# Reordering the opening loads and the first pairs' schedule of a fused attention and feed-forward kernel

## The chip, the cores and the metric

The kernel runs on one core of one Trainium2 chip. The metric is device microseconds of that core, from the run's own clock; the span in the profile, from the first to the last instruction, is 1.7 to 2.1 us shorter in most runs. All runs quoted here are fast runs, with a mean granted clock of 0.990 to 1.000. The kernel before takes 418.2 us.

The engines' names in the profile: PE is TensorE's matmuls, PEld its weight loads, DVE is VectorE, ACT is ScalarE, POOL is GpSimd and SP is SyncE; PEq, ACTq and SPq are sequencers, which issue DMAs among other things.

## The reference

```python
# q, k, v: (8 batches, 8 heads, 576, 64); bias_table: (32 buckets, 8 heads)
scores = scale * np.matmul(q, k.transpose(0, 1, 3, 2))
...                                   # bucket = function of |i - j| only
bias = bias_table[bucket]
scores = scores + bias.transpose(2, 0, 1)[None, :, :, :]
attn = softmax(scores)                # written out in the original
x = (attn @ v).transpose(0, 2, 1, 3).reshape(4608, 512)
a = x @ moe_w_a                       # 512 x 1536
b = x @ moe_w_b
return (a * b) @ moe_w_out            # 1536 x 512
```

## The kernel before

The work is cut into 32 "pairs" of heads, four to a batch. For each pair, TensorE turns q and k (transposes), makes four 128-row blocks of scores (`qk1`) and the scores of the last 64 rows (`qk_tail`). ScalarE takes their exponential (`ex`, `ex_tail`), VectorE multiplies by the exponentiated bias `W` (`mul`), TensorE multiplies by the values (`av`), VectorE divides by the row sums (`norm`). From pair 4 on, slices of the feed-forward part, called units (`U`), are put between these steps. The order on every engine is fixed by the program.

The program uses eight banks of PSUM: two score tiles of two banks each (`ps_sc`), one for value products (`AV`), one for transposes (`TR`), two for the feed-forward part (`FF`). The exponentials go into a ring of eight tiles.

```python
atp   = ctx.enter_context(tc.tile_pool(name="atp", bufs=8))      # exponentials
ps_sc = ctx.enter_context(tc.tile_pool(name="ps_sc", bufs=2, space=PSUM))
...
nc.sync.dma_start(out=bt_sb[0:NB, :], in_=bias_table)            # bias table first
nc.scalar.dma_start(out=oh_sb[0:NB, :], in_=oh_handle.ap())      # one-hot of the buckets
make_identity(nc, id32[:, :])
...
load32(0, q, q32, (nc.sync, nc.scalar))                          # pair 0
load32(0, k, k32, (nc.sync, nc.scalar))
...
warm_up(5)
nc.tensor.matmul(out=tps[0:H, 0:NR], lhsT=bt_sb[0:NB, :], rhs=oh_sb[0:NB, :], ...)
warm_up(3)
nc.scalar.activation(out=tab_sb[...], in_=tps[...], func=ACTF.Exp)
nc.scalar.dma_start(out=tab.ap(), in_=tab_sb[0:H, :])            # to HBM ...
load_w(nc.gpsimd, 0)                                             # ... and back as W
...
for s in (1, 2):                       # pairs 1 and 2, still without feed-forward
    if s > 1:
        ex(s, 0)
    mul(s - 1, 3); mul_tail(s - 1)
    q_next(s);  qk1(s, 2); ex(s, 1)
    k_next(s);  qk1(s, 3); ex(s, 2)
    tails_next(s + 1, 1, ACT)          # last 64 rows of the next pair
    qk_tail(s); mul(s, 0)
    av(s - 1, 0); av(s - 1, 1); av(s - 1, 2); norm(s - 1, 0)
    mul(s, 1);  ex(s, 3)
    av(s - 1, 3, FF)
    qk1(s + 1, 0)                      # the next pair's first scores
    ex_tail(s); av(s - 1, 4); norm(s - 1, 3)
    mul(s, 2);  qk1(s + 1, 1)
...
# pairs 5 to 11, one step list each
    steps += [lambda: qk(s, 2), lambda: ex(s, 2)]
    if e:
        steps += [lambda: t_q(s + 1, TR), lambda: c_q(s + 1)]
    steps += [U, lambda: ex(s, 3), U, lambda: mul(s, 2)]
    if e:
        steps += [lambda: t_k(s + 1, TR), lambda: c_k(s + 1)]    # same bank as qktt
```

The softmax here doesn't subtract the row's maximum and nothing guards it: scores larger than these inputs give would overflow.

Of the kernel before, what the change touches and what calls it, by code (L numbers as in the profile page):

```python
# [13 lines left out]
def kernel(  # L14
# [11 lines left out]
    nc = tc.nc  # L26
# [6 lines left out]
    NB = 32  # L33
# [132 lines left out]
        eng.dma_start(out=W_sb[hp][:, :, :],  # L166
                      in_=bass.AP(tensor=tab, offset=2 * hp * TB, ap=[[1, 128], [TB, 2], [1, 384]]))

    nc.sync.dma_start(out=bt_sb[0:NB, :], in_=bias_table)
    nc.scalar.dma_start(out=oh_sb[0:NB, :], in_=oh_handle.ap())  # L170
    make_identity(nc, id32[:, :])
    def pad(eng, x, n):
        eng.memset(x[0:64, :, 1, 0:n], 0.0)
# [6 lines left out]
    def load32(p, src, out, engs):  # L180
        for h in range(2):
            load_h(engs[h], src, out[:, p, :, h, :], 0, 2 * p + h)

    load32(0, q, q32, (nc.sync, nc.scalar))
    load32(0, k, k32, (nc.sync, nc.scalar))
    load32(1, q, q32, (nc.sync, nc.sync))
    load32(1, k, k32, (nc.sync, nc.sync))

# [64 lines left out]
    def copy(eng, out, in_):  # L253
        if eng is nc.scalar:
            nc.scalar.activation(out=out, in_=in_, func=ACTF.Copy)
        else:
            nc.vector.tensor_copy(out=out, in_=in_)  # L257
# [21 lines left out]
    def bank(where, dt, name):  # L279
        return where[0].tile([128, 512 if dt is FP32 else 1024], dt, tag=where[1], name=name)  # L280
# [5 lines left out]
    def t_q(p, where):  # L286
        if p >= NP or not early(p // 4):
            return
        ps = bank(where, BF16, f"trq{p}")
        for t in range(NM):  # L290
            nc.tensor.transpose(ps[:, 128 * t:128 * t + 128], blocks(qn, p)[:, t, :, :], ident)  # L291
        st[p]["q"] = ps
# [13 lines left out]
    def t_k(p, where):  # L306
        if p >= NP or not early(p // 4):
            return
        ps = bank(where, BF16, f"trk{p}")
        for t in range(NM):  # L310
            nc.tensor.transpose(ps[:, 128 * t:128 * t + 128], blocks(kn, p)[:, t, :, :], ident)
        if p > 4:
            t_tails(p, ps, SM)
        st[p]["k"] = ps
# [265 lines left out]
    def t32(ps, src, p, t):  # L580
        nc.tensor.transpose(ps[:, 128 * t:128 * t + 128], src[:, p, t, :, :], id32[:, :])

    psk0, psq0 = bank(FF, FP32, "trk0a"), bank(TR, FP32, "trq0a")
    psq1, psk1 = bank(AV, FP32, "trq0b"), bank(FF, FP32, "trk0b")
    t32(psk0, k32, 0, 0)
    for t in range(NM):
        t32(psq0 if t < 2 else psq1, q32, 0, t)
    copy(ACT, QT[0][:, 0:256], psq0[:, 0:256])
    copy(None, KT[0][:, 0:128], psk0[:, 0:128])
    for t in range(1, NM):  # L590
        t32(psk1, k32, 0, t)
    copy(None, QT[0][:, 256:512], psq1[:, 256:512])
    copy(None, KT[0][:, 128:SM], psk1[:, 128:512])
    qk1(0, 0)
    qk1(0, 1, 1)
# [35 lines left out]
    load32(3, k, k32, (nc.sync, nc.sync))  # L631
    qk1(0, 3)
    ex(0, 2)
    tails_next(0, 2, None)
    qk1(1, 0)
    ex(0, 3)
    ex(1, 0)
    qk_tail(0)
# [5 lines left out]
    for s in (1, 2):  # L644
        if s > 1:
            ex(s, 0)
        mul(s - 1, 3)
        mul_tail(s - 1)
        q_next(s)
        qk1(s, 2)  # L650
        ex(s, 1)
        k_next(s)
        qk1(s, 3)
        ex(s, 2)
        tails_next(s + 1, 1, ACT)
        qk_tail(s)
        mul(s, 0)
        av(s - 1, 0)
        av(s - 1, 1)
        av(s - 1, 2)  # L660
        norm(s - 1, 0)
        mul(s, 1)
        ex(s, 3)
        av(s - 1, 3, FF)
        qk1(s + 1, 0)
        ex_tail(s)
        av(s - 1, 4)
        norm(s - 1, 3)
        mul(s, 2)
        qk1(s + 1, 1)  # L670
# [18 lines left out]
    ex(3, 2)  # L689
    av(2, 3, FF)  # L690
    av(2, 4)
    c_x(1)
    norm(2, 3)
    ex_tail(3)
    qk1(3, 3)
    mul(3, 0)
    ex(3, 3)
    t_x(2, FF)
    mul(3, 1)
    av_part(3, 0)  # L700
    c_x(2, ACT)
    t_q(4, FF)
    c_q(4, ACT)
    mul(3, 2)
    av_part(3, 1)
    mul_tail(3)
    av_part(3, 2)
    av_part(3, None)
    mul(3, 3)
    av_part(3, 3)  # L710
    t_k(4, FF)
    c_k(4, ACT)
    norm(3, 0)
    norm(3, 3)
# [1 line left out]
    t_x(3, AV, range(3))  # L716
    t_x(3, AV, range(3, 5))
    ff_mm(0, 0, wb_sb, "pb", 0, 3)
    c_x(3)

    def tails4():
        ps = bank(TR, BF16, "trt4")
# [15 lines left out]
    for s in range(4, NP + 1):  # L738
        new = s < NP
        U = "unit"  # L740
        A = lambda *jq: (lambda: [av(s - 1, j, AV if j < 3 or s >= R3 else TR) for j in jq])
        N = lambda j: (lambda: norm(s - 1, j))
        steps = []
        if s == R3:
            ring3 = True
        if s == 4:
            steps += [U, U, lambda: qk1(4, 0), lambda: ex(4, 0), lambda: qk1(4, 1), U, lambda: ex(4, 1),
                      lambda: qk1(4, 2), U, lambda: ex(4, 2), lambda: qk1(4, 3), lambda: ex(4, 3),
                      lambda: mul(4, 0), U, tails4, U, lambda: qk_tail(4), lambda: ex_tail(4),
                      lambda: mul(4, 1), U, lambda: mul(4, 2), U, lambda: mul(4, 3),  # L750
                      lambda: mul_tail(4), U, lambda: t_q(5, TR), lambda: c_q(5), U,
                      lambda: t_k(5, TR), lambda: c_k(5), U, U]
        elif new:
            e = early((s + 1) // 4)
            steps += [lambda: qk(s, 0), lambda: ex(s, 0), U, lambda: ex(s, 1), A(0, 1, 2), N(0), U,
                      lambda: mul(s, 0)]
            av34 = [A(3, 4), N(3)]
            if s - 1 in XD:
                av34 += [lambda: t_x(s - 1), lambda: turns(s)]
            if s < R3:  # L760
                steps += av34
            steps += [U, lambda: mul(s, 1)]
            if s >= R3:
                steps += av34
            steps += [lambda: qk(s, 2), lambda: ex(s, 2)]
            if e:
                steps += [lambda: t_q(s + 1, TR), lambda: c_q(s + 1)]
            steps += [U, lambda: ex(s, 3), U, lambda: mul(s, 2)]
            if e:
                steps += [lambda: t_k(s + 1, TR), lambda: c_k(s + 1)]  # L770
            steps += [U, lambda: mul(s, 3), lambda: qk_tail(s), lambda: ex_tail(s), U]
            if s - 1 not in XD:
                steps += [lambda: t_x(s - 1, TR), lambda: c_x(s - 1), lambda: turns(s)]
            steps += [U, lambda: mul_tail(s), U]
        else:
            steps += [A(0, 1, 2), N(0), U, A(3, 4), N(3), U, lambda: t_x(s - 1, AV),
                      lambda: c_x(s - 1), U, U, U, U, U, U, U]
        quota = quotas.get(s, 9)
        seen, put = 0, 0
        nu = sum(1 for x in steps if x is U)  # L780
        for x in steps:
            if x is U:
                seen += 1
                n = (quota * seen + nu - 1) // nu - put
                put_units(n)
                put += n
            else:
                x()
        b = s // 4 + 1
        if new and s % 4 == 2 and b + 1 < B:  # L790
            load_qkt(b + 1)
        if new and 2 <= b < B:
            if s % 4 == 0:
                load_v(b)
                if b % 2 == 0:
                    load_vt(b, 2)
# [31 lines left out]
```

## Time and profile before

| | before |
|---|---|
| time, median of 4 runs | 418.23 us (418.14 to 418.42) |
| span of the profiled run, granted clock | 416.6 us, 1.000 |
| busy: TensorE, ScalarE, VectorE, GpSimd | 403.1, 245.3, 197.5, 119.3 us |
| first exponential | 7.63 us |
| first feed-forward matmul | 30.91 us |
| first exponential of pair 10 | 94.44 us |

TensorE is busy 97% of the span, so with the same matmuls the kernel can only lose or win where TensorE has to wait. The holes that this change touches are in the first 95 us: the opening, pairs 0 to 3 without feed-forward work to fill holes, and pairs 4 to 11 with their own transposes.

### The profile page before, as it was taken

The numbers are of one execution on the slowest core, as the hardware profiler recorded it, in microseconds if no ns is written. First come the engines' busy times: TensorE is split into PE (matmuls) and PEld (weight loads), VectorE is DVE, ScalarE is ACT, GpSimd is POOL, SyncE is SP. The second block draws the span as 40 slices with busy tenths as digits, with TensorE's granted clock in tenths as the row PEclk, the third lists the DMA queues.
The fourth block names the chain that finished last, engine by engine and source line by source line (L and its number), as shares of the span: only waits on it lengthen the run. The fifth ranks groups of instructions, "written<-read, shape, count | busy, mean of one in ns | idle before, by whom it ended". The sixth has DMA issues, their size and how long they took to land.

```text
span 416.6 us, 8424 instructions
## 1 busy us (share of the span) xinstructions
PE 403.1 (97%) x3350; PEld 207.2 (50%) x3407; DVE 197.5 (47%) x485; ACT 245.3 (59%) x345; POOL 119.3 (29%) x161
## 2 busy tenths in 40 slices
PE   8799999999999999999999999999999999999996
PEld 3573555555445555545544555555545554444443
DVE  4685666556542565255535553455425540330430
ACT  4887565766656766677666665666567642322321
POOL 9898839904528000920073003000000000000000
PEclk9999999999999999999999999999999999999999
DMA  9999999997949960999099907921120002002004
GB/s 157 196 152 176 164 169 146 180 151 99 123 60 158 177 60 17 152 177 122 16 110 200 127 14 74 173 53 39 40 90 4 14 17 101 2 0 101 2 0 101
DMA packets 164935, 40.75 MB, mean 98 GB/s; under 512 B 155320, under 2 KB 160224, under 8 KB 164896
## 3 DMA queue, kind: packets, MB, share of 16 engines
q0 software_dynamic: 110448, 18.75, 64.0%
q1 hardware_dynamic: 53168, 21.03, 27.3%
q10 hardware_dynamic: 1280, 0.43, 0.5%
q8 instruction: 26, 0.43, 0.4%
q14 instruction: 13, 0.11, 0.1%
HBM read 38.77 MB, written 9.45 MB: 116 GB/s over the span
## 4 chain that ended last, share of the span: by engine, by line
PE 90%; DVE 3%; DMA 2%; POOL 2%; issue 2%; ACT 0%; POOLq 0%; DVEq 0%; ACTq 0%
PE pa L511 22%; PE pb L511 22%; PE po L542 21%; PE av L412 9%; PE qk L342 7%; PE av L403 2%; PE qkt L367 1%; DMA kn<-in_k_dram 1%; PE qkt L370 1%; DMA W<-bias_tab 1%; PE qktt L373 1%; PE po L530 1%; PE trx L475 1%; DVE KT L257 1%; DVE XG L449 1%
## 5 line engine op out<-in xcount | busy, mean ns | idle before, releaser
L353 ACT ACTIVATE at<-qk 128x1024 bf16<-128x1024 f32 x128 | 126.2, 1023 | 24.4 <-PE qk L342 24.4
L523 DVE TENSOR_TENSOR g<-pb,ha 128x512 bf16<-128x512 f32 x108 | 74.7, 691 | 118.2 <-PE pb L511 105.1
L511 PE MATMUL pa<-xn,wa 128*128 128x512 bf16 x417 | 110.1, 380 | 1.1 <-issue 0.3
L511 PE MATMUL pb<-xn,wb 128*128 128x512 bf16 x411 | 109.1, 379 | 1.1 <-issue 0.2
L518 ACT ACTIVATE ha<-pa 128x512 f32<-128x512 f32 x108 | 64.6, 598 | 66.6 <-PE pa L511 66.1
L542 PE MATMUL po<-wo,g 128*128 128x512 bf16 x403 | 96.3, 379 | 1.1 <-issue 0.3
L511 PEld LDWEIGHTS <-wa 128*128 128x128 bf16 x432 | 39.3, 98 | 49.7 <-issue 8.8
L511 PEld LDWEIGHTS <-wb 128*128 128x128 bf16 x432 | 39.4, 98 | 46.7 <-issue 5.8
L361 DVE TENSOR_TENSOR at<-at,W 128x512 bf16<-128x512 bf16 (+1 forms) x128 | 59.1, 483 | 7.4 <-ACT at L353 5.5
L542 PEld LDWEIGHTS <-g 128*128 128x128 bf16 x420 | 37.9, 98 | 46.3 <-issue 7.4
L546 ACT ACTIVATE ob<-po 128x512 f32<-128x512 f32 x35 | 20.9, 597 | 60.7 <-PE po L542 58.8
L123 POOL DMA_DIRECT2D vm<-in_v_dram x32 | 28.2, 923 | 98.2 <-PE av L412 61.0
L412 PE MATMUL av<-vm,at 128*128 128x65 bf16 x992 | 43.3, 193 | 0.0
L412 PEld LDWEIGHTS <-at 128*128 128x128 bf16 x992 | 39.4, 97 | 6.3
L448 DVE RECIPROCAL rc<-av 128x6 f32<-128x6 f32 x64 | 12.0, 187 | 54.2 <-PE av L412 52.4
L403 PE MATMUL av<-vt,att 128*128 128x130 bf16 x156 | 34.7, 222 | 0.0
L381 ACT ACTIVATE att<-qkt 128x1024 bf16<-128x1024 f32 x32 | 32.6, 1020 | 0.0
L449 DVE TENSOR_TENSOR XG<-av,rc 128x384 bf16<-128x384 f32 x64 | 31.4, 491 | 2.4 <-DVE rc L448 0.2
L123 POOL DMA_DIRECT2D qn<-in_q_dram x28 | 24.4, 920 | 24.5 <-PE trq L291 17.2
L123 POOL DMA_DIRECT2D kn<-in_k_dram x28 | 24.5, 912 | 5.0 <-DMA vt<-in_v_dram 2.3
L342 PE MATMUL qk<-QTb,KTb 64*128 64x512 bf16 x160 | 24.2, 381 | 0.0
L403 PEld LDWEIGHTS <-att 128*128 128x128 bf16 x156 | 15.3, 98 | 7.4 <-issue 0.7
(121 smaller groups left out, 239.6 us busy)
## 6 DMA issues: line engine op xcount, KB each, us to landing
out_dram<-ob SPq DMA_DIRECT2D x32, 256.0 KB, 4.2
vm<-in_v_dram POOLq DMA_DIRECT2D x28, 128.0 KB, 5.7
qn<-in_q_dram POOLq DMA_DIRECT2D x24, 128.0 KB, 8.9
kn<-in_k_dram POOLq DMA_DIRECT2D x24, 128.0 KB, 10.2
wa<-in_moe_w_a_dram POOLq DMA_DIRECT2D x3, 512.0 KB, 7.7
wb<-in_moe_w_b_dram POOLq DMA_DIRECT2D x3, 512.0 KB, 9.8
wo<-in_moe_w_out_dram POOLq DMA_DIRECT2D x1, 1536.0 KB, 13.1
W<-bias_tab POOLq DMA_DIRECT2D x4, 192.0 KB, 5.8
```

What stands on the lines that cost most here:

```text
L123: nc.gpsimd.dma_start(out=(vm[b % 2][:, h0:h1, t, 0:Dh] if dst is None else dst[b % 2][:, :].rearrange("p (t h d) -> p t h d", h=H, t=NM)[ ...
L342: nc.tensor.matmul(out=ps[:, hh, :], lhsT=kT_(p, t)[r, :], rhs=qT[r, :, :], start=True, stop=True)
L353: nc.scalar.activation(out=at[:, :, :], in_=ps[:, :, :], func=ACTF.Exp, scale=scale)
L361: nc.vector.tensor_tensor(out=at[:, :, lo:hi], in0=at[:, :, lo:hi], in1=w[:, :, y:(None if z < 0 else z):-1], op=MULT)
L381: nc.scalar.activation(out=at[:, 0:1024].rearrange("p (a x) -> p a x", a=2), in_=ps[:, :, :], func=ACTF.Exp, scale=scale)
L403: nc.tensor.matmul(out=pav[:, slot, :, :], lhsT=x, rhs=vt[b // 2 % 2][:, 4 * i + hp, :, 0:Dh + 1], start=fresh, stop=True, skip_group_chec ...
L412: nc.tensor.matmul(out=pav[:, slot, hh, :], lhsT=x, rhs=vm[i][:, 2 * hp + hh, t, 0:Dh + 1], start=False, stop=True, skip_group_check=True)
L449: nc.vector.tensor_tensor(out=xg[:, j0:j0 + n, :, :], in0=pav[:, 0:n, :, 0:Dh], in1=rc.unsqueeze(3).to_broadcast([128, n, 2, Dh]), op=MULT)
L511: nc.tensor.matmul(out=ff[key][:, :], lhsT=w[df // FW][:, mc, 128 * (df % FW):128 * (df % FW) + 128], rhs=xn_sb[mc][:, xin(c)], start=(i = ...
L518: nc.scalar.activation(out=ha[:, :], in_=ff["pa"][:, :], func=ACTF.Copy)
L523: nc.vector.tensor_tensor(out=g_sb[df][:, :], in0=ff["pb"][:, :], in1=ff["ha"][:, :], op=MULT)
L542: nc.tensor.matmul(out=po[:, :], lhsT=g_sb[df][:, 128 * tt:128 * tt + 128], rhs=wo_sb[:, df, :], start=(df == 0), stop=(df == NDF - 1))
```

## The change

Its words name four intents: the next pair's first scores go behind one group of value products instead of four, pair 4 is turned in a score bank, the key transposes go to the value bank (so that the tail scores and they no longer share one), and the copies of the tails go from ScalarE to VectorE. The diff also does something that the words don't name: the identity and the four loads of pair 0 stand twice, and the two loads of the table come behind both.

```diff
-    nc.sync.dma_start(out=bt_sb[0:NB, :], in_=bias_table)
-    nc.scalar.dma_start(out=oh_sb[0:NB, :], in_=oh_handle.ap())
     make_identity(nc, id32[:, :])
 ...
     load32(0, q, q32, (nc.sync, nc.scalar))
     load32(0, k, k32, (nc.sync, nc.scalar))
+    make_identity(nc, id32[:, :])
 ...                                       # pad, ones, load32 defined again
+    load32(0, q, q32, (nc.sync, nc.scalar))
+    load32(0, k, k32, (nc.sync, nc.scalar))
+    nc.sync.dma_start(out=bt_sb[0:NB, :], in_=bias_table)
+    nc.scalar.dma_start(out=oh_sb[0:NB, :], in_=oh_handle.ap())
 ...                                       # pair 0: the four turns of q before k's,
                                           # k's first copy on ScalarE
+    qk1(1, 0)
     tails_next(0, 2, None)
-    qk1(1, 0)
 ...                                       # pairs 1 and 2
-        tails_next(s + 1, 1, ACT)
+        tails_next(s + 1, 1, None)
 ...
         av(s - 1, 0)
+        ex(s, 3)
+        qk1(s + 1, 0)
         av(s - 1, 1)
         av(s - 1, 2)
         norm(s - 1, 0)
         mul(s, 1)
-        ex(s, 3)
         av(s - 1, 3, FF)
-        qk1(s + 1, 0)
 ...                                       # pair 3; pair 4's q and k turned
+    sc4 = ps_sc.tile([128, 2, 1024], BF16, tag="sc", name="tr4")
+    t_q(4, sc4[:, 0, :])
+    t_k(4, sc4[:, 1, :])
 ...
-    c_x(3)
+    copy(ACT, xn_sb[3][:, 0:384], st[3]["x"][:, 0:384])
+    copy(None, xn_sb[3][:, 384:SM], st[3]["x"][:, 384:SM])
+    copy(None, xn_sb[3][:, xc(0)[1]], st[3]["x"][:, SM:S])
 ...                                       # pairs 4 to 11 (t_k(5) also to AV)
-            steps += [lambda: qk(s, 2), lambda: ex(s, 2)]
+            steps += [lambda: qk(s, 2), lambda: ex(s, 2), U]
 ...
-            steps += [U, lambda: ex(s, 3), U, lambda: mul(s, 2)]
+            steps += [lambda: ex(s, 3), U, lambda: mul(s, 2)]
             if e:
-                steps += [lambda: t_k(s + 1, TR), lambda: c_k(s + 1)]
+                steps += [lambda: t_k(s + 1, AV), lambda: c_k(s + 1)]
```

More of the change, by code (lines that the diff above doesn't have):

```diff
@@ L185, with pad, ones, load32 @@
     load32(0, k, k32, (nc.sync, nc.scalar))
+    make_identity(nc, id32[:, :])
+    def pad(eng, x, n):
+        eng.memset(x[0:64, :, 1, 0:n], 0.0)
+        eng.memset(x[64:128, :, 0, 0:n], 0.0)
+    def ones(eng, x):
+        eng.memset(x[0:64, :, 0, Dh:Dh + 1], 1.0)
+        eng.memset(x[64:128, :, 1, Dh:Dh + 1], 1.0)
+    def load32(p, src, out, engs):
+        for h in range(2):
+            load_h(engs[h], src, out[:, p, :, h, :], 0, 2 * p + h)
+    load32(0, q, q32, (nc.sync, nc.scalar))
+    load32(0, k, k32, (nc.sync, nc.scalar))
+    nc.sync.dma_start(out=bt_sb[0:NB, :], in_=bias_table)
+    nc.scalar.dma_start(out=oh_sb[0:NB, :], in_=oh_handle.ap())
     load32(1, q, q32, (nc.sync, nc.sync))
@@ L288, in t_q @@
             return
-        ps = bank(where, BF16, f"trq{p}")
+        ps = bank(where, BF16, f"trq{p}") if type(where) is tuple else where
         for t in range(NM):
@@ L308, in t_k @@
             return
-        ps = bank(where, BF16, f"trk{p}")
+        ps = bank(where, BF16, f"trk{p}") if type(where) is tuple else where
         for t in range(NM):
@@ L584 @@
     psq1, psk1 = bank(AV, FP32, "trq0b"), bank(FF, FP32, "trk0b")
-    t32(psk0, k32, 0, 0)
     for t in range(NM):
         t32(psq0 if t < 2 else psq1, q32, 0, t)
+    for t in range(NM):
+        t32(psk1 if t else psk0, k32, 0, t)
     copy(ACT, QT[0][:, 0:256], psq0[:, 0:256])
-    copy(None, KT[0][:, 0:128], psk0[:, 0:128])
-    for t in range(1, NM):
-        t32(psk1, k32, 0, t)
     copy(None, QT[0][:, 256:512], psq1[:, 256:512])
+    copy(ACT, KT[0][:, 0:128], psk0[:, 0:128])
     copy(None, KT[0][:, 128:SM], psk1[:, 128:512])
@@ L691 @@
     av(2, 4)
-    c_x(1)
     norm(2, 3)
@@ L697 @@
     ex(3, 3)
-    t_x(2, FF)
+    sc4 = ps_sc.tile([128, 2, 1024], BF16, tag="sc", name="tr4")
+    t_q(4, sc4[:, 0, :])
+    t_k(4, sc4[:, 1, :])
     mul(3, 1)
     av_part(3, 0)
-    c_x(2, ACT)
-    t_q(4, FF)
-    c_q(4, ACT)
+    c_x(1, ACT)
     mul(3, 2)
@@ L706 @@
     mul_tail(3)
+    t_x(2, FF)
+    c_x(2, ACT)
     av_part(3, 2)
@@ L710 @@
     av_part(3, 3)
-    t_k(4, FF)
+    c_q(4, ACT)
     c_k(4, ACT)
@@ L751 @@
                       lambda: mul_tail(4), U, lambda: t_q(5, TR), lambda: c_q(5), U,
-                      lambda: t_k(5, TR), lambda: c_k(5), U, U]
+                      lambda: t_k(5, AV), lambda: c_k(5), U, U]
         elif new:
```

## The prediction

> **What bounds the kernel now.** I read the page first, then the windows of 5 us and the timeline of each engine over the first 100 us, then the chain and the DMA view.
>
> ```profile
> span 416.6 us, 8424 instructions
> ...
> PE   8799999999999999999999999999999999999996
> ...
> POOL 9898839904528000920073003000000000000000
> ...
> DMA  9999999997949960999099907921120002002004
> ```
>
> Each digit is a fortieth of the span, 10.4 us. TensorE is full everywhere, so from the first feed-forward matmul (31 us) on, a microsecond comes only from a hole between matmuls. The start is different: in the window 12.5 to 30 us ScalarE is busy 16.95 of 17.5 us, because the exponentials follow each other. And in the first 90 us the DMA row is full and POOL, which issues the loads, nearly so: the loads are a second, almost critical stream. The opening, from the timeline (start, duration, engine):
>
> ```profile
> 0.76 0.41 ACTq L170 DMA_DIRECT2D oh_sb<-oh  x1
> ...
> 1.22 0.43 SPq L129 DMA_DIRECT2D q<-in_q_dram  x1
> ...
> 1.78 0.53 ACTq L129 DMA_DIRECT2D k<-in_k_dram  x1
> ...
> 3.44 1.02 PE L217 MATMUL tab_ps<-oh_sb,bt_sb 32*8 32x256 f32 x2
> ...
> 4.39 0.98 PE L212 MATMUL warm<-zero_sb 128*128 128x512 bf16 x3
> ...
> 5.92 0.30 PE L581 MATMUL trk0a<-id,k 128*128 128x128 f32 x1 [0.54 <-DMA k<-in_k_dram]
> ```
>
> The bias-table product stands ahead of the first transposes in TensorE's queue, and those wait 0.54 us for the first k. The DMA view of 0 to 20 us gives issue to landing (last figure):
>
> ```profile
> q<-in_q_dram ACTq DMA_DIRECT2D x1, 128.0 KB, 3.4
> k<-in_k_dram ACTq DMA_DIRECT2D x1, 128.0 KB, 4.0
> ...
> oh_sb<-oh ACTq DMA_DIRECT2D x1, 32.0 KB, 1.9
> ```
>
> The chain of waits shows the two places where the load stream is on the path:
>
> ```profile
> 9.44 4.58 DMA W<-bias_tab
> ...
> 66.36 5.30 DMA kn<-in_k_dram
> 71.66 0.05 issue
> 71.71 0.23 PE trk L311
> ```
>
> At 71.7 us the key transposes of pair 8 start the moment their load has landed. Last, the holes that the change aims at, in ScalarE's and TensorE's timelines (bracket: idle before, and who ended it):
>
> ```profile
> 12.44 1.02 ACT L353 ACTIVATE at<-qk 128x1024 bf16<-128x1024 f32 x1 [1.04 <-PE qk L342]
> ...
> 16.26 0.38 ACT L255 ACTIVATE KT<-trt 128x256 bf16<-128x256 f32 x1
> ```
> ```profile
> 72.11 0.38 PE L370 MATMUL qkt<-QT,KT 128*128 128x512 bf16 x1
> 72.70 0.22 PE L373 MATMUL qktt<-KT 128*128 128x64 bf16 x2 [0.21 <-DVE KT L257]
> ```
>
> A 512-column matmul releases TensorE after about 0.22 us (0.86 us for four in the chain), so the second start could be 72.33: a hole of 0.37 us. qktt and the key transposes share one PSUM bank, and qktt waits until VectorE has emptied it.
>
> **What the Trainium skill says.** "DMA: Bandwidth & Descriptors", Anatomy of one DMA: a DMA has a fixed cost of about 2.0 us, mostly the receipt of the last byte, and semaphore waits happen on the issuing sequencer before dispatch. The trace agrees: the 32 KB table took 1.9 us. The same page, Issuing engines are not separate DMA queues: all issuers share the 16 DMA engines; here 128 KB loads took 3.4 to 4.0 us among others. "TensorE: Matmul & The Clock Gate", What's actually happening: after an idle window of about 3.4 us TensorE falls to half clock. The first five warming matmuls (2.31 us, 0.46 each) and the later 0.22 us agree.
>
> **The change, part by part.** The first hunk is not a pure move. The identity and the four loads of pair 0's q and k now stand twice, and the bias table and one-hot loads come after both. The instruction order of the built kernel, with waits, confirms it: on SP and ACT each second load waits for the landing of the first into the same tile, and the table loads queue behind. That gives:
> - First q issues at 0.75 instead of 1.21, a gain of 0.46. It lands at about 0.75 + 3.4 = 4.1, first k at 1.3 + 3.8 = 5.1.
> - Second q issues at 4.1. Second k issues at 5.2 on the same queue and lands, at 3 to 3.6 us with less beside it, at 8.2 to 8.8.
> - One-hot issues behind it at 5.7. By 1.9 us it could land at 7.6, but it sits behind k in the same queue: I take 8.4.
> - Table product 1.0 us to 9.4; three warming matmuls, by then cold (idle 3.5 to 8.4), 3 x 0.43 = 1.3; transposes start at 10.7 against 5.92: **+4.8 us** on the compute path.
> - Exponential and store of the table 9.8 against 4.90. In the old trace SP sees that store landed at 8.67, 3.8 us after issue. So W's load issues at about 13.2 instead of 9.44: **+3.8 us** on the POOL queue, which stands still behind it. By bytes: 4 x 128 KB more at the 220 GB/s or so of these slices is 2.4 us, plus some 1.2 us of empty queues between the two rounds, 3.6 less 0.46. I choose a shift of the load stream of **+3.4**, range 2.5 to 4.2.
>
> What is won back on the compute path:
> - Pair 1's first scores ahead of the tail transposes: the 1.04 us hole before 12.44 closes, **-1.0**.
> - Two tail copies leave ScalarE. Each holds it 0.28 us (16.26 to the next exponential at 16.54): **-0.6**. VectorE has the room, 14.40 of 17.5 us busy, but there the copy queues behind multiplies that wait for W.
> - Next pair's scores after one group of value products: they only feed ScalarE earlier; I count the 0.48 us hole before 27.12 as half closed, **-0.25**.
> - Pair 4 turned in a score bank, transposes of x after the first value products: TensorE stands 0.33 us at 28.1 and 0.37 us at 31.8 on VectorE's norms. One goes and VectorE loses 0.43 us of copies: **-0.5**. The copies moved to ScalarE lie in its idle 2.5 us between 30 and 33.4.
> - Key transposes in the value bank: by start-to-start times qktt loses 0.53, 0.37, 0.37, 0.37 and 0.31 us at 53, 63, 72, 80 and 91 us, and the query transposes 0.36 at 60 on the same bank. The first three of these, 1.63 with the 0.36, lie before 72 us, **-1.6**; the rest **-1.05** after it.
>
> At 72 us the compute path is then +4.8 - 1.0 - 0.6 - 0.25 - 0.5 - 1.6 = +0.85. But the load of pair 8's k is +3.4, and it was already the last to arrive. TensorE's queue is static, so it must wait there: about 2.5 us of new idling, spread over the first loads that were just in time. (Pair 6's last k piece is another: issued at 48.43 with 3.2 us to landing, so 51.63, and its transposes start at 51.75.) So the shift at 72 us is the stream's, +3.4, and what was won before is lost in that wait. After it only -1.05 counts: +3.4 - 1.05 = +2.35. After 95 us nothing changes that I can see: holes over 0.13 us there are mostly of 0.22, which are missing records. 418.2 + 2.35 = **420.5 us**.
>
> **The rivals.**
> 1. *The duplicate loads are hidden and the change does what it says.* For: the loads before were only 0.54 us late. Against: waits for a landing are in the built order, and the table product blocks TensorE's queue. It would give -0.46 - 1.0 - 0.6 - 0.25 - 0.5 - 1.6 - 1.05, some -5.4 us: 412.8, still within 2%. I give it one in thirty.
> 2. *The load stream catches up, so compute alone sets the end.* For: between 54.59 and 62.84 POOL issues nothing, waiting for the output weights' landing, so an issuing delay could vanish. Against: the data itself is back to back there, and late bytes stay late. It would give +0.85 - 1.05 = -0.2: 418.0. One in ten.
> 3. *The late W adds to the late transposes.* The tail copy on VectorE stands behind four multiplies that need W (14.12 to 16.8 before), and the tail scores of pair 1 wait for it. With W at 17.8, they start at about 21 instead of 16.4, +4.6, and the exponentials with them. It would surface only if the stream's shift is small; or, with a stream of +4.2 and no gain on the bank, 422.5. One in seven.
>
> **Range and chances.** The span of the stream's shift, 2.5 to 4.2, less 1.05 gives 419.7 to 421.4; the second rival pulls the low end to 418.6, the third the high end to 422.3. Being 2% off needs 8.4 us either way. Slower needs every delay of the start to add and nothing won; faster needs more than all holes I found.
>
> **What would show it.** In the changed profile: two rounds of q and k loads, the second issued at 4 to 5 us; table product at 8 to 9 us; first transposes near 10.7; W's load issued at about 13.2; no idle of 1 us on ScalarE between its fourth and fifth exponentials; qktt no longer waiting for KT; TensorE idle on DMA kn, together 1.5 to 3 us, between 50 and 76 us. I am wrong if the first transposes start before 8 us, if W's load still issues before 11 us, or if no matmul waits for a load at 50 to 76 us and the end is later all the same.

## More of the kernel before

The prediction shows the page and the holes on ScalarE. One view that it didn't show decides this case: the chain of waits of the kernel before between 20 and 27 us, that is pair 2's tail scores and pair 1's value products (start, duration, engine, tile and line):

```profile
21.95 0.22 PE qktt L373 x2
...
23.13 0.24 PE av L412 x8
23.37 0.32 PE qk L342 x2
23.70 0.16 PE av L403
23.86 0.24 PE av L412 x8
24.10 0.32 PE qk L342 x2
```

One matmul follows the other. ScalarE is nearly full there as well, but the chain runs on TensorE and touches VectorE little: in the 15 us from 16 to 31 us its pieces sum to 12.02 us of TensorE and 2.75 us of VectorE.

## The result, and the profile after

| | before | after |
|---|---|---|
| time, median of 4 runs | 418.23 us (418.14 to 418.42) | 422.51 us (422.23 to 422.99) |
| ratio of fast runs, 95% interval | | 1.0103 (1.0085 to 1.0120) |
| profiled span, granted clock | 416.6 us, 1.000 | 420.5 us, 0.998 |
| busy: TensorE, VectorE | 403.1, 197.5 us | 403.5, 196.8 us |
| read from HBM | 38.77 MB | 39.29 MB |

A ratio here is the mean time of one kernel's fast runs over the mean of the other's fast runs of the same rounds, so it is not quite the ratio of the medians quoted beside it. The changed kernel is 1.0% slower: within 2%, as expected, but 422.51 us lies just above the range, and the loss of 4.28 us is almost twice the 2.3 us predicted.

The page of the changed kernel; a digit is a fortieth of the span:

```profile
span 420.5 us, 8435 instructions
...
PE   4899999999999999999999999999999999999996
...
POOL 8688866920808200840055003000000000000000
...
q10 hardware_dynamic: 2336, 0.70, 0.7%
```

Of TensorE's row only the first two digits have changed: the first from 8 to 4, so some 4 us of idling are in the first 10.5 us, and the second from 7 to 8. GpSimd's row is a little thinner there too. Queue 10, ScalarE's, moved 0.43 MB before and 0.70 MB now, which is two more loads of 128 KB; the other two of the four are on SP's queue.

The timeline of the first 16 us after (start, duration, engine, line; in brackets the idle time before and what ended it):

```profile
3.45 0.37 SPq L129 DMA_DIRECT2D q<-in_q_dram  x1
...
5.20 0.53 ACTq L200 DMA_DIRECT2D oh_sb<-oh  x1
...
8.21 1.01 PE L232 MATMUL tab_ps<-oh_sb,bt_sb 32*8 32x256 f32 x2 [4.70 <-DMA oh_sb<-oh]
...
9.16 1.46 PE L227 MATMUL warm<-zero_sb 128*128 128x512 bf16 x3
...
10.41 0.63 PE L596 MATMUL trq0a<-id,q 128*128 128x128 f32 x2
...
12.90 4.69 ACT L368 ACTIVATE at<-qk 128x1024 bf16<-128x1024 f32 x5 [0.91 <-PE qk L357]
```

The second loads go out only when the first into the same tile have landed, and the one-hot matrix behind them is issued at 5.20 instead of 0.76 us. TensorE stands 4.70 us for it, since the table's product comes first in its order; the second loads of q (6.30 us) and k (7.73 us) had landed before it. It then works at half speed for a while: the three warming matmuls take 1.46 us instead of 0.98, and the transposes stand 0.21 us apart instead of 0.11. The idling isn't shown to be the reason: six runs with the opening of the kernel before (e3, e4, e6, e7, e10, e12) have no idle time there and take the same 1.46 us. The chain of waits of the same stretch says it shortest:

```profile
1.29 3.49 DMA k<-in_k_dram
4.80 0.37 ACTq L129
5.20 2.97 DMA oh_sb<-oh
8.21 1.01 PE tab_ps L232 x2
```

The hole of 1.04 us ahead of ScalarE's fifth exponential, shown in the prediction, is closed: after, the first five run without a break. It closes in e2 too (below), where only the opening is changed, so the new order isn't what closed it. The hole stood for a load: TensorE's timeline before, and ScalarE's of e2:

```profile
11.43 0.30 PE L618 MATMUL trt<-id,kt 128*128 128x128 f32 x1 [1.12 <-DMA kt<-in_k_dram]
```
```profile
13.01 4.98 ACT L368 ACTIVATE at<-qk 128x1024 bf16<-128x1024 f32 x5 [1.23 <-PE qk L357]
```

The tail transposes, ahead of pair 1's first scores, waited 1.12 us for the tail of k to land. With the start 5 us later that load is in time, whatever the order. What ScalarE's timeline shows in place of such holes, after:

```profile
18.25 0.22 ACT L395 ACTIVATE att<-qktt 128x64 bf16<-128x64 f32 x1 [0.66 <-PE qktt L388]
...
23.54 3.77 ACT L368 ACTIVATE at<-qk 128x1024 bf16<-128x1024 f32 x4 [0.37 <-PE av L427]
...
28.84 1.94 ACT L368 ACTIVATE at<-qk 128x1024 bf16<-128x1024 f32 x2 [0.49 <-PE av L427]
31.14 1.02 ACT L368 ACTIVATE at<-qk 128x1024 bf16<-128x1024 f32 x1 [0.36 <-PE qk L357]
```

The first exponentials of pairs 2 and 3 ran without a recorded wait before:

```profile
18.61 2.85 ACT L353 ACTIVATE at<-qk 128x1024 bf16<-128x1024 f32 x3
...
23.74 2.91 ACT L353 ACTIVATE at<-qk 128x1024 bf16<-128x1024 f32 x3
```

So holes were closed and others opened. Why is in the chain after, at the place that answers to the one shown of before:

```profile
22.23 0.35 PE qk L357 x2
...
23.33 0.21 DVE rc L463
...
23.56 0.56 DVE XG L464
24.12 0.47 DVE at L376
...
24.71 0.42 DVE XG L464
25.14 0.80 DVE at L376 x2
...
26.76 0.69 DVE KT L272
...
27.50 0.39 PE qk L357 x2
```

The scores at 22.23 us now stand ahead of the value products that the norm (`rc`, `XG`) needs. From 23.33 to 27.45 us the end hangs on VectorE: norm, multiplies, norm, multiplies, the copies of the next QT and KT, and only then the next scores. In the 15 us from 21 to 36 us the chain's pieces sum to 5.77 us of VectorE (2.75 before) and 7.13 us of TensorE.

In the list of waits (engine, line, awaited; us in total, times, longest us), 17.5 to 36 us after:

```profile
DVE rc L463 <- PE av L427: 2.4, 4, 1.4
...
DVE at L376 <- DMA W<-bias_tab: 0.5, 1, 0.5
```

and 12.5 to 30 us before:

```profile
DVE at L361 <- DMA W<-bias_tab: 1.9, 2, 1.2
...
DVE rc L448 <- PE av L412: 0.9, 2, 0.7
```

VectorE's norm waits 1.5 us longer for value products, and its multiplies wait less for W, although W is 4.2 us later, because all else is later too.

At pair 8, where the prediction expected TensorE to stand for its late k, TensorE's timeline after shows:

```profile
76.35 0.39 PE L326 MATMUL trk<-cst_sb,kn 128*128 128x128 bf16 x4
...
76.91 0.38 PE L385 MATMUL qkt<-QT,KT 128*128 128x512 bf16 x1
77.12 0.22 PE L388 MATMUL qktt<-KT 128*128 128x64 bf16 x2
```

No wait for the load, and no hole ahead of the tail scores: 0.21 us start to start, where it was 0.59 before. The last k landed at 74.93 us (71.66 before).

The lag behind the kernel before, read at the start of the same instruction in both traces, for this kernel and for the experiments that the argument rests on (us; e1 to e10 are named below). Two traces with the same opening can differ by 0.5 us and more at the first exponential, from -0.71 (e8) to +0.55 us (e4), as TensorE comes to full speed earlier or later; from pair 1 on that evens out to 0.2 us in most (at pair 2, e9 and e11 are 0.56 and 0.34 us behind).

| at the start of | after | e1 | e2 | e3 | e4 | e6 | e7 | e10 |
|---|---|---|---|---|---|---|---|---|
| pair 0, first exponential | +5.28 | +2.79 | +5.39 | +0.54 | +0.55 | +0.07 | +0.10 | +0.43 |
| pair 2, first exponential | +4.94 | +2.45 | +4.52 | -0.19 | +0.17 | 0.00 | +0.18 | -0.05 |
| pair 3, third exponential | +5.52 | +3.04 | +4.98 | -0.19 | +1.05 | +0.58 | +0.17 | -0.05 |
| first feed-forward product on VectorE | +5.98 | +3.50 | +4.99 | -0.19 | +1.05 | +1.03 | +0.63 | -0.04 |
| pair 7, first exponential | +5.03 | +2.55 | +4.99 | -1.14 | +1.05 | +0.09 | -0.31 | -0.98 |
| pair 10, first exponential | +3.76 | +1.28 | +4.98 | -1.83 | +0.81 | -1.19 | -1.14 | -1.78 |
| end of the span | +3.83 | +1.29 | +5.06 | -1.82 | +0.80 | -1.17 | -1.13 | -1.78 |

The column "after" in four steps: +5.28 at the start, another +0.70 until the feed-forward part starts, -2.22 from there to pair 10, +0.07 to the end. The second step hides a part: e2, with the opening alone, falls from +5.39 to +4.99 by the same point, so the new early order costs 5.98 - 4.99 = 0.99 us. e6, which has that order without the opening, agrees with 1.03.

### The profile page after: what moved, and what is told of

Read it like the earlier page. It is cut to its first block, busy times and chain, and to the rows that moved or that the text cites. A ratio compares the mean times of both kernels' runs of the same rounds, so it can differ in the third digit from the quotient of the medians.

```text
span 420.5 us, 8435 instructions
## 1 busy us (share of the span) xinstructions
PE 403.5 (96%) x3350; PEld 208.2 (50%) x3407; DVE 196.8 (47%) x484; ACT 246.0 (58%) x347; POOL 119.9 (29%) x163
## 3 DMA queue, kind: packets, MB, share of 16 engines
HBM read 39.29 MB, written 9.45 MB: 116 GB/s over the span
## 4 chain that ended last, share of the span: by engine, by line
PE 93%; DVE 2%; DMA 2%; ACT 1%; issue 1%; ACTq 0%
PE pa L526 22%; PE pb L526 22%; PE po L557 22%; PE av L427 9%; PE qk L357 8%; PE av L418 2%; PE qkt L382 2%; PE qkt L385 1%; DMA k<-in_k_dram 1%; DMA oh_sb<-oh 1%; DVE XG L464 1%; ACT at L368 1%; PE po L545 1%; PE qktt L388 1%; PE trx L490 1%
```

## The experiments

All twelve gave correct results. Times are medians, with the ratio to the kernel before of the same rounds and its 95% interval.

### What the opening costs: e1, e2, e6

e1 is the changed kernel without the second identity and the second loads, so that the table still comes behind q and k:

```diff
     load32(0, k, k32, (nc.sync, nc.scalar))
-    make_identity(nc, id32[:, :])
 ...
-    load32(0, q, q32, (nc.sync, nc.scalar))
-    load32(0, k, k32, (nc.sync, nc.scalar))
     nc.sync.dma_start(out=bt_sb[0:NB, :], in_=bias_table)
```

> The changed kernel with the second identity and the second q and k loads of pair 0 taken out; the rest stays, the bias table loads behind the first q and k loads too. Theory A (the duplicate sets the whole loss, by delaying the first exponential, 12.90 us against 7.63 before): first exponential near 7.2 to 7.7 us, about 5.3 us earlier than in the changed kernel. If the rest then keeps its changed distances (0.7 us lost between the first exponential and 39 us, 2.1 won after 50 us), 416.6 to 417.2 us. Theory B (the load stream is just in time before the change and holds TensorE back once compute is early): the key transposes at about 51.5 and 71.5 us wait for kn, part of the 2.1 is lost, and the time is 417.2 to 418.0. Rival (the duplicate costs little, the reordering does the damage): over 420.

Measured: 419.91 us, ratio 1.0035 (1.0022 to 1.0048), span 417.9 us. That is 2.6 us better than the changed kernel, but it misses what was expected. The duplicate was thought to be nearly the whole delay; half of it was the table's place behind the first q and k. From its timeline:

```profile
5.79 1.02 PE L217 MATMUL tab_ps<-oh_sb,bt_sb 32*8 32x256 f32 x2 [2.27 <-DMA oh_sb<-oh]
```

The one-hot matrix was issued at 1.90 us and released the product at 5.79, 3.9 us later.

e2 is the opposite, the kernel before with only the first hunk of the diff:

> The kernel before with the first hunk alone: identity and pair 0's loads twice, bias table loads behind both. Theory A (compute path delayed by the late table product): first exponential near 12.6 to 12.9 us, and no win anywhere, so 5.0 to 5.5 us over the kernel before, 423.2 to 423.8; no wait of TensorE on kn at 51 to 77 us, since compute is later than the loads. Theory of the prediction (the load stream carries the delay): about 3.3 us, 421.5. Rival (hidden): under 419.

Measured: 423.63 us, ratio 1.0123 (1.0110 to 1.0136), span 421.7 us. The lag of +4.5 to +5.4 us from the opening stays to the end, and the time is the one that Theory A expected. But e2 can't tell compute and loads apart, since its loads are as late as its compute. Two pieces of load are on its chain of waits after the opening, the third W and pair 8's last k:

```profile
20.21 7.45 DMA W<-bias_tab
...
68.63 0.45 PE qktt L388 x2
...
70.83 5.81 DMA kn<-in_k_dram
...
76.69 0.23 PE trk L326
```

W landed at 27.66 us (21.39 before), VectorE stood 1.14 us for it, and the lag goes from 4.52 to 4.98 between pair 3's first and third exponential. The last k landed at 76.64 us, 4.98 us later than before and not 3.4, because its issue in turn had waited for TensorE; the four key transposes take 0.61 us there, as they did before (0.62). That loads don't set the time is shown in the changed kernel: its chain has none after the one-hot matrix, and at pair 8 the transposes start 1.42 us after the last k has landed.

e6 is the changed kernel with the whole first hunk undone:

> The changed kernel with its whole first hunk undone: no duplicates, and the two table loads ahead of q and k again. Theory A (TensorE's queue puts the table product before the first transposes, so table loads behind q and k delay everything even without the duplicate): table product at 3.4 to 3.5 us instead of 5.79 in e1_dedupe, first exponential at 7.6 to 8.2 instead of 10.42, and 2.3 to 2.8 us less than e1_dedupe: 417.1 to 417.6. Rival (the first hunk without its duplicate is neutral or a small gain, as the prediction took it, and the other 1.3 us of e1_dedupe's loss come from the rest of the change): 419.6 to 420.4.

Measured: 417.91 us, ratio 0.9975 (0.9962 to 0.9989), span 415.5 us, table product back at 3.44 us. (That is a little above the 417.1 to 417.6 expected; the kernel before took 418.79 us in these rounds.) e2's +5.06 and e6's -1.17 sum to +3.89, against +3.83 for the two together: opening and rest add up, and the loss is all in the opening.

### What the early order costs: e4, e5, e7

e4 is the kernel before with the next pair's first scores moved ahead, alone:

```diff
         av(s - 1, 0)
+        ex(s, 3)
+        qk1(s + 1, 0)
         av(s - 1, 1)
         av(s - 1, 2)
         norm(s - 1, 0)
         mul(s, 1)
-        ex(s, 3)
         av(s - 1, 3, FF)
-        qk1(s + 1, 0)
```

> The kernel before with only this moved, in the steps of pairs 1 and 2: the fourth exponential and the next pair's first scores ahead of the second group of value products. Theory A (the next pair's first exponential writes a buffer of the ring of eight that the previous pair's value products still read, and these now stand behind the scores): ScalarE stands 0.3 to 0.6 us ahead of each of two exponentials, released by the value products, and the first feed-forward matmul comes 0.3 to 0.8 us later; 418.3 to 419.0. Rival (the move is a win, as meant): 0.25 to 0.5 us earlier, 417.7 to 418.0.

Measured: 419.31 us, ratio 1.0023 (1.0011 to 1.0035), span 417.4 us. The lag grows from -0.31 us (pair 1) to +0.17 at pair 2 and +1.05 at the end of pair 3: the move costs 1.36 us, in a kernel in which nothing else is changed. That is more than either expectation, and the mechanism that the first one names is tested in e5. VectorE's timeline, e4 first, then before, the norm of pair 1:

```profile
24.16 0.20 DVE L448 RECIPROCAL rc<-av 128x6 f32<-128x6 f32 x1 [1.16 <-PE av L412]
```
```profile
23.11 0.20 DVE L448 RECIPROCAL rc<-av 128x6 f32<-128x6 f32 x1 [0.69 <-PE av L412]
```

The norm is 1.05 us later and VectorE has stood longer for its value products. In e4 the chain of 16 to 31 us has 8.43 us of VectorE in it. In e2, e3, e5, e11 and e12 the chain of this stretch runs through the loads. In the others it tells the two orders apart, over 15 us each: with the new one 5.77 us of VectorE in the changed kernel and in e1, 8.43 in e4, 6.79 in e6; with the old one 2.75 before, 1.19 in e7, 2.42 in e8, 1.73 in e9 and 1.95 in e10.

e5 asks whether the wait "[0.37 <-PE av]" of ScalarE, which is for a free tile of the ring of exponentials, is the cause. It is e1 with a longer ring:

```diff
-    atp = ctx.enter_context(tc.tile_pool(name="atp", bufs=8))
+    atp = ctx.enter_context(tc.tile_pool(name="atp", bufs=10))
```

> The kernel of e1_dedupe with ten instead of eight buffers for the exponentials' outputs. Theory A (the reordering costs because the next pair's first exponential overwrites a buffer that the previous pair's value products still read): the idle times of ScalarE of 0.37 and 0.50 us ended by the value products go, and the next pair's first exponentials come 0.3 to 0.9 us earlier; 419.0 to 419.6 us against 419.9. Rival (TensorE's own order delays the scores, whatever buffer they go to): the first exponentials of pairs 2 and 3 at the same distances as in e1_dedupe within 0.1 us, and 419.7 to 420.1.

Measured: 420.11 us, ratio 1.0032 (1.0020 to 1.0045), so no better than e1. ScalarE's timeline of e5:

```profile
20.77 1.09 ACT L353 ACTIVATE at<-qk 128x1024 bf16<-128x1024 f32 x1
22.03 2.86 ACT L353 ACTIVATE at<-qk 128x1024 bf16<-128x1024 f32 x3 [0.17 <-PE qk L342]
```

The first exponential of pair 2 is 0.29 us earlier than in e1 (20.77 against 21.06), the second is not (22.03 against 21.98). The wait was real, and taking it away moved it one instruction on, to the next scores. It was a symptom.

e7 is e6 with the old order of pairs 1 and 2:

> As e6_table_first, with the order of pairs 1 and 2 as it was before (value products together, next pair's first scores after them). Theory A (the reordering costs 1.0 to 1.4 us, as it did alone on the kernel before): 1.0 to 1.5 us less than e6_table_first, 415.8 to 416.4. Rival (loads just in time at 51 and 71 us take back what compute wins): less than 0.5 us gained, and waits of TensorE on kn appear.

Measured: 417.24 us, ratio 0.9960 (0.9947 to 0.9972). That misses the 415.8 to 416.4 expected; the rival's sign appears. At pair 7 its trace is 0.40 us ahead of e6's, at the end level with it, since now a load does bind. TensorE's timeline of e7:

```profile
71.61 0.23 PE L311 MATMUL trk<-cst_sb,kn 128*128 128x128 bf16 x1 [0.27 <-DMA kn<-in_k_dram]
```

The intervals of e6 and e7 overlap, so that e7 is the faster of the two isn't shown; the order's cost at the spot is.

### What the other early parts are worth: e9, e8, e11, e10

e9 is the kernel before with the last copy of pair 3 split over ScalarE and VectorE:

```diff
-    c_x(3)
+    copy(ACT, xn_sb[3][:, 0:384], st[3]["x"][:, 0:384])
+    copy(None, xn_sb[3][:, 384:SM], st[3]["x"][:, 384:SM])
+    copy(None, xn_sb[3][:, xc(0)[1]], st[3]["x"][:, SM:S])
```

> The kernel before with only the last copy of x (pair 3) split into a part for ScalarE and two for VectorE. Theory A (the parts run one after the other: VectorE waits for ScalarE's, the first product of pair 3's block comes later): fourth exponential of pair 3 to first product on VectorE 6.2 us against 5.91 before, and 0.2 to 0.4 us slower in the span. Rival (split shares the work): 5.7 us and 0.2 us faster.

Measured: 418.65 us, ratio 1.0011 (0.9997 to 1.0024): not told from 1 by time, but in the trace the stretch from the last exponential of pair 3 to VectorE's first feed-forward product takes 6.23 us instead of 5.91. VectorE's timelines, e9 and then before:

```profile
33.63 0.32 DVE L257 COPY xn<-trx 128x128 bf16<-128x128 bf16 x2 [0.90 <-ACT xn L255]
```
```profile
32.55 0.52 DVE L257 COPY xn<-trx 128x512 bf16<-128x512 bf16 x2 [0.38 <-PE trx L475]
```

VectorE's two small copies wait 0.90 us and start after ScalarE's large one: split over two engines, the parts ran one after the other. In the trace the first of them waits for the semaphore that ScalarE's copy sets, so the built program asks for this turn.

e8 takes the split out of e7 again (one `c_x(3)`):

> As e7_table_first_old_order, with the last copy of x (pair 3) on VectorE alone as before, instead of split between ScalarE and VectorE. Theory A (the two halves run one after the other, since VectorE waits for ScalarE's): first product of the feed-forward about 0.3 us earlier after the last transposes, 0.2 to 0.4 us less than e7: 415.5 to 416.1. Rival (the split helps by sharing the copy): 0.1 to 0.3 us more. Against the kernel before: 0.5 to 0.7% faster.

Measured: 417.87 us, ratio 0.9973 (0.9961 to 0.9986), so no better than e7. At the spot it won what e9 lost (6.05 us instead of e7's 6.37). But the profiled run was slow earlier on: in the table by windows (window, length, then busy us of PE, PEld, DVE, ACT and POOL, granted clock, DMA engines busy, GB/s):

```profile
12.00:13.00 1.00, 0.48 (x5) 0.31 (x5) 0.76 (x2) 0.00 (x0) 1.00 (x3) 0.50 1.09 155
```

From 11.9 to 18.7 us the clock stood at 0.50, after a stretch in which TensorE was busy 57% (8.5 to 11.9 us); no gap from 3.4 us on was over 1.01 us. This trace can't be used for the sum, therefore; why the clock fell in it is open. It doesn't explain the time either: the other four runs, at mean clocks of 0.998 to 1.000, took 416.78 to 417.93 us. That e8 missed its 415.5 to 416.1 stays open.

e11 puts pair 1's first scores ahead of the tails' transposes, on top of e3 (below):

```diff
+    qk1(1, 0)
     tails_next(0, 2, None)
-    qk1(1, 0)
```

> The kernel of e3_late_only with pair 1's first scores ahead of the tail transposes. Theory A (the wait moves: the tail scores still need the tails turned and copied, so ScalarE stands ahead of the tail exponentials instead of ahead of pair 1's first): the idle of about 1 us before pair 1's first exponential goes, one of 0.6 us or more appears before the first tail exponential, and pair 3's first exponential comes at most 0.4 us earlier; time within 0.4 us of e3. Rival (the hole closes, as predicted): 1.0 us earlier throughout.

Measured: 418.28 us (416.86 to 419.32), ratio 0.9995 (0.9971 to 1.0018), where within 0.4 us of e3 was expected. The time is a poor measure here: two of the four runs lie 3.1 and 3.5 us above their spans, and the spans are 415.1 to 416.3 us, within those of e3. The trace is read instead. The fifth exponential starts 1.51 us earlier than before, the sixth 0.21 us. ScalarE's timeline of e11 shows where the difference went:

```profile
13.13 0.22 ACT L380 ACTIVATE att<-qktt 128x64 bf16<-128x64 f32 x1 [1.16 <-PE qktt L373]
```

The hole of 1.04 us became one of 1.16 us ahead of the next instruction, the tail exponential, which waits for the tail scores. By pair 2 the trace is 0.34 us behind, which is no more than the spread: e9, unchanged up to there, is 0.56 us behind.

e10 puts the tails' copies on VectorE, on top of e3:

```diff
-        tails_next(s + 1, 1, ACT)
+        tails_next(s + 1, 1, None)
```

> The kernel of e3_late_only with the tail copies of pairs 2 and 3 on VectorE. Theory A (W's landing bounds the first pairs: multiplies, then key, query and tail copies stand behind it on VectorE, so the 0.28 us taken off ScalarE twice is lost again): fourth exponential of pair 1 0.3 us earlier than in e3_late_only, but the first exponential of pair 3 within 0.2 us of it, and the time within 0.3 us of e3. Rival (ScalarE is the bound there, as the prediction took it): pair 3's first exponential 0.5 to 0.6 us earlier.

Measured: 416.86 us (416.20 to 417.14), ratio 0.9962 (0.9948 to 0.9975), the lowest median of all. But its copies did next to nothing: the fourth exponential is 0.41 us early in pair 1, and the next pair's first only 0.05; in pair 2 again 0.51, then 0.05. The end of its trace is 0.04 us from e3's. What ScalarE gains, it waits for at the next scores.

### What the late part is worth: e3, e12

e3 is the kernel before with only the change to pairs 4 to 11: the key transposes in the value bank, and one unit moved.

```diff
-                      lambda: t_k(5, TR), lambda: c_k(5), U, U]
+                      lambda: t_k(5, AV), lambda: c_k(5), U, U]
 ...
-            steps += [lambda: qk(s, 2), lambda: ex(s, 2)]
+            steps += [lambda: qk(s, 2), lambda: ex(s, 2), U]
 ...
-            steps += [U, lambda: ex(s, 3), U, lambda: mul(s, 2)]
+            steps += [lambda: ex(s, 3), U, lambda: mul(s, 2)]
 ...
-                steps += [lambda: t_k(s + 1, TR), lambda: c_k(s + 1)]
+                steps += [lambda: t_k(s + 1, AV), lambda: c_k(s + 1)]
```

> The kernel before with only the steps of pairs 4 to 11 changed: key transposes in the value bank, one unit ahead of the query transposes. Theory A (the bank wait is what is won): the waits of the small tail scores on KT are gone and 2.0 to 2.4 us are won, 415.9 to 416.2. Theory B (loads are just in time): the transposes of pair 6 near 51.7 us and pair 8 near 71.5 us wait for kn, 0.5 to 1.3 us in all, and about 1.0 us is won, 417.1 to 417.4.

Measured: 417.17 us, ratio 0.9974 (0.9959 to 0.9990). Its trace gains 1.63 us between the feed-forward's start and pair 10, where the changed kernel gains 2.22. TensorE's timeline of e3 shows the difference at pair 8:

```profile
70.93 0.23 PE L311 MATMUL trk<-cst_sb,kn 128*128 128x128 bf16 x1 [0.42 <-DMA kn<-in_k_dram]
```

Here the load is the last to arrive: compute is 1.13 us ahead of the kernel before and the load only 0.78. Start to start the wait costs 0.58 us, which matches the gap between 1.63 and 2.22. The time is the one that Theory B expected. How much of the gain is the bank's and how much the moved unit's wasn't tested apart: the holes of the tail scores that stood for the shared bank are 1.95 us of the 2.31 listed, and the hole of the query transposes at 60 us is the rest. The six runs of e3 have spans from 414.7 to 416.6 us; why they spread more than the others isn't settled.

e12 tries to remove that wait by issuing pair 8's k earlier: the output weights come in four loads instead of one, and the next batches' tails ahead of them.

```diff
-        nc.gpsimd.dma_start(out=wo_sb[:, :, :], in_=moe_w_out.rearrange(...))
+        for i in range(4):
+            nc.gpsimd.dma_start(out=wo_sb[:, 3 * i:3 * i + 3, :],
+                                in_=moe_w_out[384 * i:384 * i + 384, :].rearrange(...))
 ...
+    load_tails(2, 2)
     load_w_out()
 ...
-    load_tails(2, 2)
```

> A version meant to beat both: the kernel of e3_late_only with the output weights loaded in four pieces and the tails of batches 2 and 3 ahead of them, so that pair 8's k loads wait for small pieces on the eight load semaphores and not for one of 1.5 MB. Theory B (the load of pair 8's k takes back 0.4 to 0.6 us of the 2.1 that the free bank wins): no wait of TensorE on kn near 70 us, span 0.4 to 0.6 us below e3_late_only, 414.2 to 414.5, and time 416.5 to 416.9. Rival (DMA bytes, not issue, set the landing): k lands at 70.5 us or later, the wait stays, and the span is 414.7 to 415.2.

Measured: 417.81 us, ratio 0.9984 (0.9971 to 0.9997), no better than e3. From its chain of waits:

```profile
63.95 7.21 DMA kn<-in_k_dram
```

The last k was issued at 63.95 us (66.38 in e3) and landed at 71.16 (70.88 in e3). An earlier issue bought nothing: the load took 7.21 us instead of 4.50. So the issue doesn't set the landing here; that the bytes ahead of it in the stream do is likely, but not shown.

## Why the prediction was right or wrong

**The opening: right.** Table product at 8.21 us (8.4 expected), first transposes at 10.41 (10.7), lag at the first exponential +5.28 (+4.8). The half microsecond is TensorE's halved speed on the transposes and first scores after the warming matmuls, which the sum had only for the warming. It is partly the luck of the two traces: e3, e4 and e10, whose opening is the old one, are 0.43 to 0.55 us late at the same place, with the transposes 0.21 us apart as well. By pair 2 the opening alone (e2) is 4.52 us late.

**The load stream: right in size, wrong in effect.** W's load was issued at 14.05 us (13.2 expected; the prediction's own store at 9.8 us plus 3.8 us to land gives 13.6), pair 8's last k landed 3.27 us later than before (3.4 expected; that the size fits is partly luck, as with the opening alone, e2, it is 4.98). But no matmul waited for it, where 1.5 to 3 us of waits were named as the sign. In the kernel before, its transposes had stood 0.23 us longer over the four (0.62 us against 0.39) for that landing; in the changed kernel even this is gone, since compute is 5.0 us late there and the load 3.3. The second rival said that compute alone sets the end, and it did. But its reason, a stream that catches up, was wrong (the stream stayed 3.3 us late), and its figure of 418.0 was off mainly by the term that failed the prediction.

**The step that failed** is the sum "+4.8 - 1.0 - 0.6 - 0.25 - 0.5 - 1.6 = +0.85". Its four early gains, together -2.35, are +0.70 in the trace (from +5.28 to +5.98), and a loss of 1.0 us when the opening is taken out (e2, e6). So compute at pair 8 was 5.0 us late and not 0.85, and the wait for k that the prediction built on this had no room. Term by term:

| term | predicted | measured |
|---|---|---|
| first scores ahead of the tails | -1.0 | nothing: a load's hole, which the late opening fills by itself. Lag at the fourth, fifth and sixth exponential: 5.69, 4.52, 4.51 in e2, with the opening alone; 5.28, 4.11, 4.91 in the changed kernel, where a new hole stands ahead of the tail exponential (0.66 us). In e11, with the old opening, nothing is left by pair 2 |
| tails' copies on VectorE | -0.6 | -0.36 and -0.46 at the spot in e10, given back by the next pair's first exponential |
| next scores behind one group of value products | -0.25 | +1.36 alone (e4); +0.41 between e7 and e6 at pair 3's third exponential |
| pair 4 in a score bank, x turned later, copy split | -0.5 | +0.46, of which +0.32 is the split (e9) |

With the +0.41 the terms sum to 0.87 of the 1.0 us, with e4's +1.36 to 1.82: they act on the same waits and don't simply add. Behind most of them stands one reading. ScalarE was busy 16.95 of 17.5 us, so the holes ahead of its exponentials were counted at face value. Yet from 17 us on the chain of waits before runs mainly through TensorE: ScalarE's holes closed, and its next instruction then waited for scores (e5, e10, e11). And moving scores ahead of the value products took from VectorE's norm what it waits for, so that 4 us in one piece of VectorE's work came onto the path (the chains of e4 and of the changed kernel). TensorE (16.14 of 17.5 us) and VectorE (14.40) were nearly as full as ScalarE there.

**The bank: right.** -2.22 us from the feed-forward's start to pair 10. The prediction's -1.6 - 1.05 = -2.65 counts the hole at 72 us in both terms; the holes that it lists, 0.53 + 0.36 + 3 x 0.37 + 0.31, sum to 2.31. (So its +0.85 should have been +1.22, and the first two rivals' figures shift by the same 0.37; the 420.5 doesn't change.) The prediction let only 1.05 of it count, because of the wait that wasn't there. All of it counted in the changed kernel; 1.63 counts in e3, where the load does bind.

So the predicted +2.35 was 3.4 - 1.05, and the measured +3.83 is 5.28 + 0.70 - 2.22 + 0.07. The predicted figure came as near as it did by luck, because two errors had opposite signs: early gains that didn't exist, and a wait that swallowed them and didn't exist either.

**The third rival** gave 422.5 us (its terms sum to 422.4), which is the figure measured, but not by its way. It had the multiplies waiting for a late W; in the changed kernel they waited 0.5 us, less than before, and off the chain. In e2 the late W did add its half microsecond. The wait for the first W is longer where compute starts on time: up to 1.2 us before, 1.29 us in e10 and 1.91 us in e7.

**The first rival**, a gain of 5.4 us with the loads hidden, fell with e2: the duplicate and the table's place cost 5.06 us to the end. Without them (e6) the rest of the change gains 1.17 us, not 5.

Both e7 and e10 beat the kernel before and the changed one, by 0.4% of the kernel before; e10 is in effect the late part (bank and moved unit) alone. One wait left in both is for pair 8's k (0.27 and 0.30 us), whose landing e12 couldn't bring forward.

## What to carry to other kernels

Before counting an engine's hole as gain, look what the hole stands for and whether the chain of waits passes through that engine there. A hole that waits for a load is filled by a later start as well, so it isn't a gain on top of the delay. A nearly full engine off the chain only hands its gain to the next wait, and an order that feeds it earlier can starve the engine behind. When a change delays both a load and the work that needs it, compare the two delays at that point; a late load costs nothing if the work is later still, and a load that waits for the work to free its tile (e2) is late with it. Where a small early load gates the first matmul of a queue with a fixed order, its place in the issue order can matter more than its size: here 32 KB moved behind 256 KB cost 2.8 us at the first exponential (e1).

## What the Trainium skill lacked or had wrong

- "DMA: Bandwidth & Descriptors", Anatomy of one DMA, gives a fixed cost of about 2.0 us and a share by bytes, for DMAs issued by GpSimd. The 32 KB one-hot load, issued by ScalarE, took 1.9 us at the head of its queue, 3.0 us in the changed kernel (5.20 to 8.17 us) and 3.9 us in e1, each time behind 128 KB loads on the same queue. That section has no figure for a small load behind larger ones.
- "TensorE: Matmul & The Clock Gate", HAM oscillation, has as its rule "no PE-idle gaps >~3.4µs". In e8 the granted clock fell to 0.50 from 11.9 to 18.7 us with no gap over 1.01 us, at 57% busy over the 3.4 us ahead; the kernel before had 67% there, with a gap of 1.12 us, and e7 85%, and both kept 1.00. One run is no rule, but the longest gap alone doesn't tell it. The page also knows a loss of clock from many short idle times, but gives no busy share at which it comes.
- The same page, Seeing it yourself, warns that clock events in traces may be unreliable. Here the granted clock reads 1.00 from 8 to 13 us of the changed kernel, while transposes of the same shape stood 0.21 us apart instead of the 0.11 of the kernel before: the durations showed the slow clock, the column didn't. The warning holds.
